# Second parts of w_out by one VectorE subtraction, first parts by ScalarE with the scale

## The chip, the cores and the metric

The kernel runs on one core of a Trainium2 chip. Four engines matter: TensorE (PE in the profile; its weight loads are PEld), VectorE (DVE), ScalarE (ACT) and GpSimd (POOL). SyncE (SP) issues the DMAs. Every engine works through its own queue in order. The metric is the device time of one execution in microseconds.

## The reference

An attention with a threshold, and behind it a feed-forward layer:

```python
scores = scale * np.matmul(q, k.transpose(0, 1, 3, 2))        # 8 batches, 8 heads, 576 x 576
thresh = np.max(scores, axis=-1, keepdims=True) - tau
scores = np.where(scores >= thresh, scores, -1000000000.0)
attn = np.exp(scores - np.max(scores, axis=-1, keepdims=True))
attn = attn / (np.sum(attn, axis=-1, keepdims=True) + 1e-09)
x = np.matmul(attn, v)                                         # as 4608 x 512
h = x @ w_in                                                   # 512 x 2048
g = h * (1.0 / (1.0 + np.exp(-h)))
out = g @ w_out                                                # 2048 x 512
```

## The kernel before

All heavy products but the scores run in float16, each operand as a pair: a first part (the value, scaled by a power of two, rounded to float16) and a second part (what the rounding left). A product is then three matmuls: first by first, first by second, second by first.

**Softmax tiles.** The work is a list of 288 tiles of 128 queries by 576 keys, nine for a pair of heads, 36 for a batch. A tile goes through scores (TensorE, L424, into one of two PSUM buffers s), maximum (VectorE, L434), exponential (ScalarE, L444), mask and sum (VectorE, L453), reciprocal (L461), scaling (ScalarE, L466), first part (GpSimd, L477), second part (GpSimd, L480 and L483), and a DMA transpose into wT. The scores of tile t+2 wait for the mask of tile t, which frees their PSUM. Once the tiles of a pair are transposed, TensorE multiplies them with v (L508, "a"). The pair of v itself is made by ScalarE (L288) and VectorE (L289) and its load needs the buffer that an earlier L289 frees.

**Feed-forward units.** For each batch and range of tokens there are 16 h units (L551: 12 matmuls with w_in, then L559 on ScalarE, L560 on VectorE, L566 on ScalarE, L567 on VectorE, which writes g into gbuf and frees the unit's PSUM bank) and 16 o units (L582: 12 matmuls with w_out each, four units to one of four output blocks; L592 on ScalarE and a DMA write a block). The first range, batch 0 with tokens 0 to 255, has 256 columns and is called h_0_0 and o_0_0; the next, h_0_256, has 320.

**Weights.** w_in and w_out arrive as 64-bit words. Each is 16 pieces of 128 x 512, decoded into float32 slots of the tile wst (L191, L194, L197). When the maxima of a matrix are known, its scale o_w_sc (or i_w_sc) is worked out on VectorE, and split_weights makes the two parts of each piece: L220 scales the piece in place on GpSimd, L223 rounds it to the first part on ScalarE, L224 subtracts on GpSimd. The parts of piece i are written two slots below the piece, over what piece i-2 was; so a first part waits until the second part of the piece two before it has been made. An o unit needs both parts of four pieces.

**Order.** The program calls these steps tile by tile. A plan says at which tile a step of the weights is called (W_PLAN: the scale of w_out is called at place 22 of the tile list and its 16 splits at places 22 to 25; the last field raises the priority of w_out's steps by 150), and how many units are put between the tiles. From these calls and priorities a scheduler that simulates the engines writes each engine's queue, so that an edit in one place reorders the queues from there on.

Of the kernel before, what the change touches and what calls it, by code (L numbers as in the profile page):

```python
# [14 lines left out]
AF = mybir.ActivationFunctionType  # L15
ALU = mybir.AluOpType
# [7 lines left out]
NK = DM // P  # L24
# [28 lines left out]
def attention_moe(  # L53
# [10 lines left out]
    nc = tc.nc  # L64
# [13 lines left out]
    def bank(shape, name, own=None):  # L78
# [10 lines left out]
        out=gate, in0=tau_sb, scalar1=0.0, scalar2=0.125, op0=ALU.is_ge, op1=ALU.mult  # L89
# [3 lines left out]
        out=ntau, in0=tau_sb, scalar1=0.0, scalar2=-1.0, op0=ALU.max, op1=ALU.mult  # L93
# [63 lines left out]
    w16 = wst.bitcast(F16)  # L157
# [58 lines left out]
    def split_weights(i):  # L216
        w = wst[:, i + WSPARE, :]
        hi = w16[:, i, 0:512]
        sc = wsc["in" if i < 4 * NK else "out"][:, 0:1]
        nc.gpsimd.tensor_scalar(  # L220
            out=w, in0=w, scalar1=sc, scalar2=1.0, op0=ALU.mult, op1=ALU.mult
        )
        nc.scalar.activation(hi, w, AF.Copy)  # L223
        nc.gpsimd.tensor_tensor(  # L224
            out=w16[:, i, 512:1024], in0=w, in1=hi, op=ALU.subtract
        )
# [472 lines left out]
    for first, t0, t1, t2, hp in W_PLAN:  # L699
        for i in range(16):  # L700
            ti = t0 + i * (t1 - t0) / 16
            at(math.floor(ti - 2), pri(hp, lambda i=i + first: load_weights(i)))
            at(math.floor(ti), pri(hp, lambda i=i + first: decode_weights(i)))
        at(t1, pri(hp, scale_out if first else scale_in))
        for i in range(16):
            at(t1 + i * (t2 - t1) // 16, pri(hp, lambda i=i + first: split_weights(i)))
# [27 lines left out]
    while t < NT + 8 or units or ready or held:  # L734
# [32 lines left out]
        for v, p, c0, n in avs.pop(t, []):  # L767
# [6 lines left out]
            scale = xscale if v in direct else 2.0**-12  # L774
# [52 lines left out]
```

## Time and profile before

| | |
|---|---|
| median of 3 runs | 1242.41 us (1241.87 to 1245.1) |
| profiled execution, its own time | 1240.96 us |
| its span | 1238.8 us |
| TensorE busy | 1142.8 us, 92% |
| VectorE busy | 931.1 us, 75% |
| ScalarE busy | 814.8 us, 66% |
| GpSimd busy | 748.6 us, 60% |

The page has, in this order, the busy time of each engine, the span in 40 slices (each digit the busy tenths of a slice of 31 us), the DMA queues, the chain of work that ended last, and the costliest groups of instructions: line, engine, operation, output<-inputs, shape, count, busy time and mean ns of one, and the engine's idle time ahead of them with what ended it. The trace behind it also gives the same by windows of time and instruction by instruction. A busy share over the whole span mixes stages with different limits: here the first 213 us, in which weights are decoded and split beside the first tiles, differ from the rest.

### The profile page before, as it was taken

Reading aid. Unit: us, or ns where it says so; the run is one execution under the profiler, and the core shown is the slowest. Engines: PE = TensorE matmul, PEld = TensorE weight load, DVE = VectorE, ACT = ScalarE, POOL = GpSimd, SP = SyncE. Lnnn points to the kernel's source line nnn. Section 1 sums busy time; section 2 is a strip of 40 time slices with the busy share of each in tenths; the row PEclk is TensorE's granted clock in tenths of the full one; section 3 lists DMA queues with packets and bytes.
Section 4 is the critical chain, followed back from the end, with each engine's and each line's share of the span. In section 5 each row is a group of like instructions: output and inputs, shape, how many; then the busy total and the mean of one; then the engine's idle time right before and its main releaser. Section 6 shows DMA issues by size and latency. Waiting matters only on the chain.

```text
span 1238.8 us, 26929 instructions
## 1 busy us (share of the span) xinstructions
PE 1142.8 (92%) x9402; PEld 896.8 (72%) x9402; DVE 931.1 (75%) x2603; ACT 814.8 (66%) x1507; POOL 748.6 (60%) x952
## 2 busy tenths in 40 slices
PE   5776766999899999999999999999999999999998
PEld 3544545777678778777777877787777877777777
DVE  7898866797989998989888859887689848333230
ACT  6888656687677867776777747776677847433331
POOL 1088999788678867886788618783688537200000
PEclk9997887999999999999999999999999999999999
DMA  9669556877878877788787648773688446200000
GB/s 303 183 208 207 129 98 131 158 135 151 163 129 151 160 150 146 154 144 162 141 153 148 123 99 146 157 148 88 118 162 154 83 79 112 52 15 15 14 12 24
DMA packets 363479, 158.15 MB, mean 128 GB/s; under 512 B 329552, under 2 KB 338256, under 8 KB 363344
## 3 DMA queue, kind: packets, MB, share of 16 engines
q1 hardware_dynamic: 363344, 156.43, 62.3%
q8 instruction: 74, 1.21, 0.4%
q14 instruction: 61, 0.50, 0.1%
HBM read 66.72 MB, written 9.44 MB: 61 GB/s over the span
## 4 chain that ended last, share of the span: by engine, by line
PE 64%; DVE 13%; DMA 8%; POOL 5%; ACT 5%; issue 3%; SPq 1%; POOLq 0%; ACTq 0%; DVEq 0%
PE h L551 23%; PE o L582 23%; PE s L424 10%; PE a L508 8%; DMA wT<-hl 3%; DVE w L453 3%; DVE sm L434 3%; DMA vraw<-in_vL 2%; DVE qstack L328 2%; POOL hl L480 2%; ACT w L444 2%; DVE v L289 1%; DMA wraw<-in_w_out 1%; POOL hl L477 1%; ACT w L466 1%
## 5 line engine op out<-in xcount | busy, mean ns | idle before, releaser
L551 PE MATMUL h<-x,wst 128*128 128x288 f16 (+2 forms) x3072 | 430.9, 289 | 14.0 <-DVE gbuf L567 12.0
L582 PE MATMUL o<-gbuf,wst 128*128 128x288 f16 (+2 forms) x3072 | 426.2, 288 | 4.9 <-ACT wst L592 2.5
L551 PEld LDWEIGHTS <-wst 128*128 128x128 f16 x3072 | 292.6, 99 | 102.8 <-issue 22.1
L582 PEld LDWEIGHTS <-wst 128*128 128x128 f16 x3072 | 294.5, 99 | 89.5 <-issue 9.1
L480 POOL TENSOR_TENSOR hl<-w,hl 128x512 f16<-128x512 f32 x272 | 325.3, 1196 | 15.7 <-DMA kraw<-in_kT 3.5
L477 POOL TENSOR_SCALAR hl<-w 128x576 f16<-128x576 f32 x264 | 178.8, 680 | 198.4 <-ACT w L466 128.3
L444 ACT ACTIVATE w<-s,sm 128x576 f32<-128x576 f32 x288 | 210.1, 737 | 81.4 <-DVE sm L434 33.8
L453 DVE SCALAR_TENSOR_TENSOR w<-s,sm,w 128x576 f32<-128x576 f32 x288 | 232.5, 812 | 41.4 <-ACT w L444 39.4
L466 ACT ACTIVATE w<-w,sm 128x576 f32<-128x576 f32 x288 | 218.4, 771 | 58.4 <-DVE sm L461 56.5
L434 DVE TENSOR_REDUCE sm<-s 128x1 f32<-128x576 f32 x288 | 215.0, 750 | 42.8 <-PE s L424 41.0
L560 DVE SCALAR_TENSOR_TENSOR h<-th,h 128x288 f32<-128x288 f32 (+2 forms) x256 | 116.5, 456 | 114.5 <-ACT th L559 112.0
L559 ACT ACTIVATE th<-h,msc 128x288 f32<-128x288 f32 (+2 forms) x256 | 126.9, 497 | 105.4 <-PE h L551 103.0
L424 PE MATMUL s<-khi,qstack 128*128 128x288 f32 x608 | 160.6, 346 | 31.3 <-DVE w L453 27.2
L566 ACT ACTIVATE gbuf<-h 128x288 f16<-128x288 f32 (+2 forms) x256 | 103.7, 407 | 81.6 <-DVE h L560 80.5
L567 DVE SCALAR_TENSOR_TENSOR gbuf<-h,gbuf 128x288 f16<-128x288 f32 (+2 forms) x256 | 114.9, 451 | 40.8 <-ACT gbuf L566 39.8
L508 PE MATMUL a<-wT,v 128*64 128x288 f16 (+1 forms) x1680 | 128.7, 295 | 10.2 <-DMA wT<-hl 10.2
L424 PEld LDWEIGHTS s<-khi,qstack 128*128 128x128 f32 x608 | 98.6, 197 | 53.8 <-issue 42.1
L338 POOL TENSOR_TENSOR klo<-kraw,khi 128x576 fp32r<-128x576 f32 x64 | 92.5, 1446 | 71.3 <-ACT khi L336 71.3
L424 PE MATMUL s<-klo,qstack 128*128 128x288 f32 x608 | 133.7, 302 | 0.0
L508 PEld LDWEIGHTS <-v 128*64 128x64 f16 x1680 | 91.3, 111 | 37.0 <-issue 25.0
L424 PEld LDWEIGHTS s<-klo,qstack 128*128 128x128 f32 x608 | 101.5, 196 | 0.5 <-issue 0.2
L483 POOL TENSOR_TENSOR hl<-w,hl 128x64 f16<-128x64 f32 x272 | 101.7, 374 | 0.0
(93 smaller groups left out, 830.6 us busy)
## 6 DMA issues: line engine op xcount, KB each, us to landing
qraw<-in_qT SPq DMA_DIRECT2D x128, 144.0 KB, 3.0
kraw<-in_kT SPq DMA_DIRECT2D x128, 144.0 KB, 3.1
vraw<-in_vL SPq DMA_DIRECT2D x32, 320.0 KB, 3.4
wraw<-in_w_out SPq DMA_DIRECT2D x16, 512.0 KB, 4.4
out_t<-wst SPq DMA_DIRECT2D x56, 144.0 KB, 2.2
wT<-hl SPq DMA_TRANSPOSE x304, 3.4
gbuf<-in_w_in SPq DMA_DIRECT2D x8, 512.0 KB, 7.5
wraw<-in_w_in SPq DMA_DIRECT2D x8, 512.0 KB, 6.0
```

What stands on the lines that cost most here:

```text
L424: nc.tensor.matmul(s_ps[:, j, :HALF], lhs, kk[:, j * HALF : (j + 1) * HALF], start=(n == 0), stop=(n == len(seq) - 1),)
L434: nc.vector.tensor_reduce(out=negm, in_=s_ps[:, :, :HALF], op=ALU.max, axis=AX.XY, negate=True)
L444: nc.scalar.activation(wtile[t].rearrange("p (j c) -> p j c", j=2), sps[t][:, :, :HALF], AF.Exp, bias=small[t][:, 0:1],)
L453: nc.vector.scalar_tensor_tensor(out=w3, in0=s_ps[:, :, :HALF], scalar=sm[:, 1:2], in1=w3, op0=ALU.is_ge, op1=ALU.mult, accum_out=sm[:, 2:3],)
L466: nc.scalar.activation(w, w, AF.Copy, scale=r)
L477: nc.gpsimd.tensor_scalar(out=fl[:, 0:S], in0=w, scalar1=1.0, scalar2=1.0, op0=ALU.mult, op1=ALU.mult)
L480: nc.gpsimd.tensor_tensor(out=fl[:, 640:1152], in0=w[:, 0:512], in1=fl[:, 0:512], op=ALU.subtract)
L508: nc.tensor.matmul(a_ps[odd * D : (odd + 1) * D, :n], vt[:, lo_v, odd, kv, :], wT[v, b * H + 2 * p + odd][:, kw, c0 - base : c0 - base + n ...
L551: nc.tensor.matmul(ph[:, :n], wi(c, f, lo_w), x16[b, lo_x][:, c, c0 : c0 + n], start=(k == 0), stop=(k == 11),)
L559: nc.scalar.activation(th[:, :n], ph[:, :n], AF.Tanh, scale=moe_sc[b][:, 0:1])
L560: nc.vector.scalar_tensor_tensor(out=ph[:, :n], in0=th[:, :n], scalar=1.0, in1=ph[:, :n], op0=ALU.add, op1=ALU.mult,)
L582: nc.tensor.matmul(ps[:, :n], wo(f, d, lo_w), g[:, lo_g, :n], start=(f == 0 and k == 0), stop=(f == NF - 1 and k == 2),)
```

## The change

For the 16 pieces of w_out the scaling on GpSimd is gone. ScalarE makes the first part from the unscaled piece with the scale as its factor, and VectorE makes the second part in one instruction, piece times scale minus first part. The pieces of w_in are treated as before. The scale is a power of two, so the parts are the same numbers.

```diff
         sc = wsc["in" if i < 4 * NK else "out"][:, 0:1]
+        if i >= 4 * NK:
+            nc.scalar.activation(hi, w, AF.Copy, scale=sc)
+            nc.vector.scalar_tensor_tensor(
+                out=w16[:, i, 512:1024], in0=w, scalar=sc, in1=hi, op0=ALU.mult, op1=ALU.subtract
+            )
+            return
         nc.gpsimd.tensor_scalar(
             out=w, in0=w, scalar1=sc, scalar2=1.0, op0=ALU.mult, op1=ALU.mult
         )
         nc.scalar.activation(hi, w, AF.Copy)
         nc.gpsimd.tensor_tensor(
             out=w16[:, i, 512:1024], in0=w, in1=hi, op=ALU.subtract
         )
```

In the changed file the new instructions are L221 (ScalarE) and L222 (VectorE), and every later line number is six higher: L480 becomes L486, L453 L459, L551 L557, L582 L588.

The queues change from there on. GpSimd before, where tile 42 comes (hl and w32 carry the tile's number, klo is a second part of k; the last number of a name only tells buffers apart):

```order
L477 TENSOR_SCALAR hl_41_1927<-w32_41_1878 128x576
L220 TENSOR_SCALAR wst_89<-wst_89,o_w_sc_996 128x512 x15
L224 TENSOR_TENSOR wst_89<-wst_89 128x512
L220 TENSOR_SCALAR wst_89<-wst_89,o_w_sc_996 128x512
L224 TENSOR_TENSOR wst_89<-wst_89 128x512
L480 TENSOR_TENSOR hl_40_1888<-w32_40_1806,hl_40_1888 128x512
L483 TENSOR_TENSOR hl_40_1888<-w32_40_1806,hl_40_1888 128x64
L480 TENSOR_TENSOR hl_41_1927<-w32_41_1878,hl_41_1927 128x512
L483 TENSOR_TENSOR hl_41_1927<-w32_41_1878,hl_41_1927 128x64
L477 TENSOR_SCALAR hl_42_1975<-w32_42_1917 128x576
```

GpSimd of the change, at the same place:

```order
L483 TENSOR_SCALAR hl_41_1911<-w32_41_1862 128x576
L486 TENSOR_TENSOR hl_40_1872<-w32_40_1790,hl_40_1872 128x512
L489 TENSOR_TENSOR hl_40_1872<-w32_40_1790,hl_40_1872 128x64
L486 TENSOR_TENSOR hl_41_1911<-w32_41_1862,hl_41_1911 128x512
L489 TENSOR_TENSOR hl_41_1911<-w32_41_1862,hl_41_1911 128x64
L483 TENSOR_SCALAR hl_42_1959<-w32_42_1901 128x576
```

The 18 rows of w_out between the first and second parts of tiles 40 and 41 are gone; the tiles follow one another.

VectorE of the change, from its first new subtraction on (th and h belong to an h unit, sm and s to a tile, v16 to a pair of v):

```order
L566 SCALAR_TENSOR_TENSOR h_0_0_8_1138<-th_0_0_8_1175,h_0_0_8_1138 128x256
L222 SCALAR_TENSOR_TENSOR wst_89<-wst_89,o_w_sc_996 128x512
L463 TENSOR_SCALAR sm_42_1900<-sm_42_1900 128x1
L275 TENSOR_TENSOR msc_1_3566<-v1_sc_2117,i_w_sc_584 128x1
L222 SCALAR_TENSOR_TENSOR wst_89<-wst_89,o_w_sc_996 128x512
L566 SCALAR_TENSOR_TENSOR h_0_0_9_1162<-th_0_0_9_1208,h_0_0_9_1162 128x256
L440 TENSOR_REDUCE sm_44_1984<-s_44_1952 128x1
L467 RECIPROCAL sm_42_1900<-sm_42_1900 128x1
```

and its last ones, ahead of the maximum of tile 51:

```order
L459 SCALAR_TENSOR_TENSOR w32_47_2092,sm_47_2091<-s_47_2070,sm_47_2091,w32_47_2092 128x576
L222 SCALAR_TENSOR_TENSOR wst_89<-wst_89,o_w_sc_996 128x512
L459 SCALAR_TENSOR_TENSOR w32_49_2141,sm_49_2140<-s_49_2123,sm_49_2140,w32_49_2141 128x576
L222 SCALAR_TENSOR_TENSOR wst_89<-wst_89,o_w_sc_996 128x512
L463 TENSOR_SCALAR sm_47_2091<-sm_47_2091 128x1
L573 SCALAR_TENSOR_TENSOR gbuf_61<-h_0_0_13_1298,gbuf_61 128x256
L566 SCALAR_TENSOR_TENSOR h_0_0_14_1345<-th_0_0_14_1400,h_0_0_14_1345 128x256
L440 TENSOR_REDUCE sm_50_2153<-s_50_2144 128x1
```

The 16 stand among the work of tiles 42 to 51, and with them the units h_0_0_14 and h_0_0_15 have moved behind those tiles. On TensorE, before, all h_0_0 units and 40 matmuls of o_0_0 stand ahead of the scores of tile 51; in the changed queue h_0_0_15 and all of o_0_0 stand behind them. Ahead of the scores of tile 59 the queue before has 94 matmuls of o_0_0 and 12 of h_0_256, the changed one 153 and 9.

## The prediction

> **What bounds the kernel now.** I read the page's busy shares and slices first.
>
> ```profile
> PE 1142.8 (92%) x9402; PEld 896.8 (72%) x9402; DVE 931.1 (75%) x2603; ACT 814.8 (66%) x1507; POOL 748.6 (60%) x952
> PE   5776766999899999999999999999999999999998
> POOL 1088999788678867886788618783688537200000
> ```
>
> TensorE is at 9 tenths from about 215 us to the end, and short of that in the first seven slices (31 us each). The windows by stage say who is short there; the columns are length, then PE, PEld, DVE, ACT and POOL busy, then granted clock and DMA.
>
> ```profile
> 20.00:40.00 20.00, 13.59 (x64) 8.90 (x64) 19.86 (x55) 18.15 (x37) 1.74 (x2) 0.83 0.86 248
> 60.00:142.00 82.00, 59.30 (x404) 43.76 (x404) 72.15 (x203) 68.91 (x132) 72.61 (x76) 0.83 0.82 192
> 142.00:184.20 42.20, 24.14 (x173) 18.68 (x172) 27.33 (x66) 24.32 (x45) 40.34 (x50) 0.86 0.48 98
> 142.00:213.00 71.00, 43.75 (x295) 33.61 (x294) 47.25 (x119) 42.17 (x74) 67.62 (x80) 0.83 0.54 108
> 213.00:300.00 87.00, 81.40 (x674) 62.62 (x672) 71.96 (x210) 63.21 (x113) 68.89 (x92) 0.98 0.80 151
> 300.00:1100.00 800.00, 781.91 (x6716) 621.42 (x6716) 654.47 (x1859) 553.88 (x1017) 535.99 (x697) 1.00 0.69 131
> ```
>
> From 142 to 213 us GpSimd is busy 67.62 of 71.00 us, TensorE only 43.75, VectorE 0.67 of the time. This is the stage of the edit, and 27.3 us of TensorE's idle time lie in it. After 213 us TensorE is busy 0.94 and then 0.98, so what this stage loses is not made up later. The chain of waits runs through the edited instructions:
>
> ```profile
> 142.02 7.97 POOL wst L220 x11
> ...
> 167.37 5.09 DMA wT<-hl
> ...
> 172.60 3.14 PE a L508 x22
> ...
> 178.44 3.58 DVE v L289
> 182.04 3.22 DMA vraw<-in_vL
> ```
>
> The block of scalings (L220) starts as tile 42 reaches GpSimd; the probabilities of tiles 40 to 42 wait behind it, then their transposes, the product with v, the next v and its load.
>
> **The change, part by part.**
>
> ```profile
> L220 POOL TENSOR_SCALAR wst<-wst,o_w_sc 128x512 f32<-128x512 f32 x16 | 12.5, 798 | 0.0
> L224 POOL TENSOR_TENSOR wst<-wst 128x512 f16<-128x512 f32 x32 | 37.8, 1192 | 0.1
> L223 ACT ACTIVATE wst<-wst 128x512 f16<-128x512 f32 x32 | 19.5, 621 | 0.6 <-POOL wst L224 0.5
> L288 ACT ACTIVATE v<-vraw,v_sc 128x640 f16<-128x640 f32 x32 | 24.5, 817 | 2.0 <-DVE v_sc L146 2.0
> L289 DVE SCALAR_TENSOR_TENSOR v<-vraw,v_sc,v 128x640 f16<-128x640 f32 x32 | 34.2, 1086 | 2.3 <-ACT v L288 2.2
> ```
>
> *Removed from GpSimd:* 16 scalings, 12.5 us, and 16 of the 32 subtractions, 16 x 1.192 = 19.1 us. Of its 67.6 us some 36 remain: it no longer bounds the stage.
>
> *ScalarE:* the first part now takes the scale from a tile, as L288 does: 817 x 512/640 = 654 ns against 621, 0.5 us over 16. At 42.17 of 71.00 us ScalarE hides that; with no cover it costs 0.5 us.
>
> *Added to VectorE:* 16 scaling subtractions. The trace of before has no such instruction on these tiles; L289 has the same operands in 640 columns. Its mean makes 1086 x 512/640 = 0.87 us, so 13.9 us. Bounds:
>
> ```profile
> L197 DVE SCALAR_TENSOR_TENSOR wst<-wraw,wst x24: 677/691/1642, 21.5 to 125.7; 128x512 int32<-128x512 int32 x24
> L289 DVE SCALAR_TENSOR_TENSOR v<-vraw,v_sc,v x4: 868/1272/3568, 143.3 to 199.3; 128x640 f16<-128x640 f32 x4
> 142.00:213.00 71.00, 6.98 (x4) 0.83 0.54 108
> ```
>
> The floor is the shortest L197 (min/median/max ns), 0.68 us; the ceiling is the longest L289, 3.568 x 0.8 = 2.85 us. The four L289 of this stage took 6.98 us (last row, that line alone), 1.40 us each at 512 columns. I take 0.87: the long ones fell where GpSimd ran without a gap, which the change ends.
>
> *Moved.* In the changed VectorE queue the 16 stand spread before the reduction of tile 51. Behind it go two L567, an L560 and an L453; ahead of it comes an L251. By the means of these rows that is 0.812 + 2 x 0.451 + 0.456 - 0.811 = 1.4 us less.
>
> ```profile
> L453 DVE SCALAR_TENSOR_TENSOR w<-s,sm,w 128x576 f32<-128x576 f32 x288 | 232.5, 812 | 41.4 <-ACT w L444 39.4
> L560 DVE SCALAR_TENSOR_TENSOR h<-th,h 128x288 f32<-128x288 f32 (+2 forms) x256 | 116.5, 456 | 114.5 <-ACT th L559 112.0
> L567 DVE SCALAR_TENSOR_TENSOR gbuf<-h,gbuf 128x288 f16<-128x288 f32 (+2 forms) x256 | 114.9, 451 | 40.8 <-ACT gbuf L566 39.8
> L251 DVE TENSOR_REDUCE vmx<-vraw 128x1 f32<-128x640 f32 x32 | 25.9, 811 | 11.0 <-DMA vraw<-in_vL 11.0
> ```
>
> *First half, 142 us to tile 51* (reduction at 184.20 us, row below). VectorE: 27.33 + 13.9 - 1.4, less 2.5 for the one L289 of 3.57 us at its mean: 37.3 us. When VectorE is the fullest engine beside a working GpSimd it is busy 72.15/82 = 0.88 (window 60 to 142). 37.3/0.88 = 42.4 us against 42.2: tile 51 comes 0.2 us later.
>
> *Second half, tile 51 to tile 59.*
>
> ```profile
> 153.08 2.80 PE L551 MATMUL h<-x,wst 128*128 128x256 f16 x24 [2.01 <-DVE gbuf L567]
> 156.51 2.80 PE L551 MATMUL h<-x,wst 128*128 128x256 f16 x24 [0.63 <-DVE gbuf L567]
> ...
> 193.75 2.09 PE L508 MATMUL a<-wT,v 128*64 128x320 f16 x28
> ...
> 196.28 0.49 PE L424 MATMUL s<-khi,qstack 128*128 128x288 f32 x2
> 196.62 0.42 PE L424 MATMUL s<-klo,qstack 128*128 128x288 f32 x2
> 196.88 1.27 PE L582 MATMUL o<-gbuf,wst 128*128 128x256 f16 x10
> ...
> 184.20 0.76 DVE L434 TENSOR_REDUCE sm<-s 128x1 f32<-128x576 f32 x1 [0.34 <-PE s L424]
> ...
> 212.99 0.76 DVE L434 TENSOR_REDUCE sm<-s 128x1 f32<-128x576 f32 x1 [0.56 <-PE s L424]
> ```
>
> The changed TensorE queue has there 153 matmuls of o and 12 of h, 28 of a and 36 of s. At 2.80/24 = 0.117 us, 2.09 us in all, and 0.60 us per four (196.28 to 196.88): 19.3 + 2.1 + 5.4 = 26.8 us. All parts of w_out exist by then, so TensorE bounds; at 81.40/87 = 0.936 busy that is 28.6 us. I add one wait of 2.0 us (row 153.08): the last h units' L567 now stand behind tile 51. Together 30.6 against 28.8: tile 59 comes 2.0 us later than before.
>
> *Work done by tile 59.* The queue before has 94 matmuls of o and 12 of h_0_256 ahead of tile 59, the changed one 153 and 9: 56 more, 56 x 0.117 = 6.6 us that need not be done later.
>
> *Sum:* 6.6 - 2.0 = 4.6 us gained. The profiled execution, 1240.96 us (span 1238.8 and 2.2 around it), becomes 1236.4; the median shown, 1.4 us higher, becomes 1237.8. It reaches the end because TensorE is busy 781.91 of 800 us from 300 us on.
>
> **Queue and port.** On VectorE's queue, behind each new subtraction, stand the masks and sums of the softmax tiles, whose PSUM the next scores wait for; behind each ScalarE first part, which waits for the subtraction two parts back (it overwrites that one's source), stand exponentials. That is the 0.88. As for contention, the long L289 (178.44 us, 3.58) ran beside these:
>
> ```profile
> 178.81 1.15 POOL L480 TENSOR_TENSOR hl<-w,hl 128x512 f16<-128x512 f32 x1
> ...
> 180.18 1.14 POOL L480 TENSOR_TENSOR hl<-w,hl 128x512 f16<-128x512 f32 x1
> 181.29 0.88 POOL L483 TENSOR_TENSOR hl<-w,hl 128x64 f16<-128x64 f32 x1
> ```
>
> The Trainium skill (SBUF — State Buffer, Who interferes with whom) says that a VectorE instruction with two SBUF inputs and a GpSimd one that reads SBUF exclude each other, the later blocking for the whole of the other. By that rule, the trace agrees: L289 got through only after two L480, and the L483 that met it took 0.88 us. An estimate by the rule: GpSimd busy 36/71 of the time, half an L480 left on average, 0.30 us on the floor of 0.68, 0.98 each; 1.8/0.88 = 2.0 us less gain, 1239.8 us.
>
> **Rivals.**
>
> *Contention, slower.* Each subtraction costs what the stage's own L289 did, 1.40 us, and L289 stays long: 16 x 0.53 + 2.5 = 11.0 us more, over 0.88 is 12.5 us: 4.6 - 12.5, 7.9 us slower, 1250.3. It decides from 0.87 + 4.6 x 0.88/16 = 1.12 us per subtraction. For it: the 6.98 us above. Against it: GpSimd falls to half busy, and the L289 of the whole run average 1.09 us with GpSimd busy 535.99 of 800 us. The rule named above is this mechanism at 0.98 us, short of the deciding point; the 1.12 us would be reached where GpSimd, behind a wait, works its queue off without a gap. The ceiling of 2.85 us would make 36 us more; it needs a GpSimd without gaps, and I leave it out.
>
> *Ping-pong, no change.* ScalarE and VectorE wait for each other through the alternating parts, and VectorE reaches only half way from its 0.67 in this stage to 0.88, 0.775: 37.3/0.775 = 48.1 us, 5.7 more: 1.1 us slower, 1243.5. For it: the parts go in pairs, each pair bound to the one before. Against it: 20 to 40 us has the two engines alternating over the same tiles at 19.86 of 20.
>
> *Denser, faster still.* VectorE at 0.99 as in 20 to 40 us and subtractions at the floor: (27.33 + 10.9 - 1.4 - 2.7)/0.99 = 34.5 us, 7.9 less: 12.5 us gained, 1229.9. Against it: GpSimd was nearly idle then.
>
> **How the numbers follow.** Chances: forecast 0.45, ping-pong 0.28, contention 0.19, denser 0.08. About 0.3%, 3.7 us, is what a measurement of this kernel tells from no change. The forecast's own range, 1234 to 1240, lies nearly all below 1238.7: 0.42 of its 0.45 count as faster, with denser 0.50. Ping-pong gives 0.25 to the same, with the forecast's rest 0.28; the other 0.03 with contention make slower 0.22. The range reaches from denser, 1229, into contention, 1247; it leaves out some 0.04 below and 0.14 above.
>
> **What would show it.** Right: GpSimd near 36 us between 142 and 213, the subtractions near 0.87 us, VectorE near 0.88 busy up to tile 51, scores of tile 59 near 215 us with o units mostly done, TensorE near 0.94 from tile 51 on. Wrong: subtractions above 1.12 us, tile 51 after 190 us, or more TensorE idle time after 300 us than the 18 of before, which would mean that the new order gives the gain back.

## The result and the profile after

The changed kernel took 1228.88 us (median of 4 runs, 1228.62 to 1229.91) beside 1242.22 for the kernel before: a ratio of 0.9889 with a 95% interval of 0.9872 to 0.9906, so 1.1% faster. A later comparison with 10 runs of it and 27 of before gave 1230.77 against 1240.60, 0.9930 (0.9913 to 0.9948). The two intervals do not meet; the gain is 10 to 13 us, where the prediction had 4.6. All ratios compare fast executions alone: one slow execution, of the kernel called "w_in too" below, took 1659.59 us at a granted clock of 0.654 and is left out of its ratio.

The page of the changed kernel, busy shares and slices. VectorE is up by 8.5 us and GpSimd down by 24.2. TensorE is at 7 and 9 tenths in slices 6 and 7, where before had 6 in both, and at 8 or 9 behind them:

```profile
PE 1142.7 (93%) x9402; PEld 896.0 (73%) x9402; DVE 939.6 (77%) x2619; ACT 816.1 (66%) x1507; POOL 724.4 (59%) x920
PE   5876779999889999998999999999999999999998
```

Windows of the changed kernel. The first two stretches run from the maximum of tile 42 (135.0 us; 135.8 before) to that of tile 51 and on to tile 59; the others are the fixed ones of the prediction. The tile list has empty places, so that VectorE takes eight maxima from tile 42 to 51 and eight from there to 59.

```profile
135.00:176.90 41.90, 26.40 (x172) 19.78 (x169) 41.74 (x100) 31.17 (x57) 27.86 (x29) 0.78 0.56 124
176.90:204.40 27.50, 27.17 (x237) 23.07 (x236) 21.52 (x64) 18.56 (x30) 22.96 (x29) 0.97 0.83 153
142.00:213.00 71.00, 55.79 (x431) 44.69 (x431) 62.59 (x156) 49.26 (x83) 51.23 (x61) 0.86 0.69 139
213.00:300.00 87.00, 84.71 (x683) 62.68 (x681) 77.17 (x223) 63.76 (x113) 66.33 (x86) 1.00 0.82 154
300.00:1100.00 800.00, 776.23 (x6658) 618.30 (x6657) 645.07 (x1833) 549.09 (x1013) 529.73 (x688) 0.99 0.67 128
```

The same two stretches of the kernel before:

```profile
135.80:184.20 48.40, 29.67 (x219) 23.01 (x218) 33.53 (x89) 28.77 (x54) 46.38 (x57) 0.88 0.49 99
184.20:213.00 28.80, 19.61 (x123) 14.93 (x124) 19.92 (x54) 17.85 (x30) 27.27 (x31) 0.78 0.62 122
```

The first stretch has changed hands. GpSimd was busy 46.38 of 48.40 us there; now VectorE is busy 41.74 of 41.90, and in the list of waits for that stretch VectorE has no entry at all. In the second TensorE is busy 27.17 of 27.50 us, before 19.61 of 28.80. TensorE's idle time from 142 to 213 us falls from 27.2 to 15.2 us and from 213 to 300 us from 5.6 to 2.3; from 300 to 1100 us it rises from 18.1 to 23.8.

The maxima of tiles 51 and 59 in the changed kernel (VectorE's timeline), 184.20 and 212.99 us before:

```profile
176.87 0.73 DVE L440 TENSOR_REDUCE sm<-s 128x1 f32<-128x576 f32 x1
...
204.37 0.74 DVE L440 TENSOR_REDUCE sm<-s 128x1 f32<-128x576 f32 x1
```

The chain of waits of the changed kernel at the place of the scaling block (start, us, work). Where GpSimd stood with L220, VectorE now stands with L222 between its other work:

```profile
140.92 0.96 DVE wst L222
141.94 0.97 DVE msc L275
142.90 0.80 DVE wst L222
...
144.99 2.01 DVE v L295 x2
...
147.46 0.73 DVE w L459 x2
148.19 1.33 DVE wst L222 x2
```

The new groups, with the idle time ahead of them behind the last bar:

```profile
L222 DVE SCALAR_TENSOR_TENSOR wst<-wst,o_w_sc 128x512 f16<-128x512 f32 x16 | 14.5, 924 | 0.0
L221 ACT ACTIVATE wst<-wst,o_w_sc 128x512 f16<-128x512 f32 x16 | 11.3, 721 | 4.7 <-DVE wst L222 4.5
```

VectorE never waited ahead of a subtraction. ScalarE waited 4.5 us in all for the subtraction two pieces back; VectorE, full all the while, did not have to wait for it.

### The profile page after: what moved, and what is told of

Read it like the earlier page. It is cut to its first block, busy times and chain, and to the rows that moved or that the text cites. A ratio compares the mean times of both kernels' runs of the same rounds, so it can differ in the third digit from the quotient of the medians.

```text
span 1228.1 us, 26910 instructions
## 1 busy us (share of the span) xinstructions
PE 1142.7 (93%) x9402; PEld 896.0 (73%) x9402; DVE 939.6 (77%) x2619; ACT 816.1 (66%) x1507; POOL 724.4 (59%) x920
## 4 chain that ended last, share of the span: by engine, by line
PE 61%; DVE 17%; DMA 7%; ACT 5%; POOL 5%; issue 4%; SPq 1%; ACTq 0%; POOLq 0%; DVEq 0%
PE o L588 22%; PE h L557 22%; PE s L430 9%; PE a L514 7%; DVE w L459 3%; DVE sm L440 3%; DMA wT<-hl 3%; DVE qstack L334 2%; DMA vraw<-in_vL 2%; POOL hl L486 2%; POOL hl L483 1%; ACT w L450 1%; DVE v L295 1%; ACT w L472 1%; DVE h L566 1%
## 5 line engine op out<-in xcount | busy, mean ns | idle before, releaser
L557 PE MATMUL h<-x,wst 128*128 128x288 f16 (+2 forms) x3072 | 435.8, 291 | 21.7 <-DVE gbuf L573 20.6
L588 PE MATMUL o<-gbuf,wst 128*128 128x288 f16 (+2 forms) x3072 | 421.5, 287 | 2.6 <-ACT wst L598 2.0
L557 PEld LDWEIGHTS <-wst 128*128 128x128 f16 x3072 | 293.3, 99 | 114.5 <-issue 31.7
L588 PEld LDWEIGHTS <-wst 128*128 128x128 f16 x3072 | 293.7, 98 | 84.3 <-issue 6.4
L486 POOL TENSOR_TENSOR hl<-w,hl 128x512 f16<-128x512 f32 x272 | 329.7, 1212 | 14.5 <-DMA kraw<-in_kT 1.8
L459 DVE SCALAR_TENSOR_TENSOR w<-s,sm,w 128x576 f32<-128x576 f32 x288 | 231.7, 813 | 30.3 <-ACT w L450 28.0
L573 DVE SCALAR_TENSOR_TENSOR gbuf<-h,gbuf 128x288 f16<-128x288 f32 (+2 forms) x256 | 115.6, 453 | 45.4 <-ACT gbuf L572 44.7
L430 PEld LDWEIGHTS s<-khi,qstack 128*128 128x128 f32 x608 | 97.6, 195 | 42.5 <-issue 29.6
```

Source lines behind the costliest of these rows:

```text
L430: nc.tensor.matmul(s_ps[:, j, :HALF], lhs, kk[:, j * HALF : (j + 1) * HALF], start=(n == 0), stop=(n == len(seq) - 1),)
L459: nc.vector.scalar_tensor_tensor(out=w3, in0=s_ps[:, :, :HALF], scalar=sm[:, 1:2], in1=w3, op0=ALU.is_ge, op1=ALU.mult, accum_out=sm[:, 2:3],)
L486: nc.gpsimd.tensor_tensor(out=fl[:, 640:1152], in0=w[:, 0:512], in1=fl[:, 0:512], op=ALU.subtract)
L557: nc.tensor.matmul(ph[:, :n], wi(c, f, lo_w), x16[b, lo_x][:, c, c0 : c0 + n], start=(k == 0), stop=(k == 11),)
L588: nc.tensor.matmul(ps[:, :n], wo(f, d, lo_w), g[:, lo_g, :n], start=(f == 0 and k == 0), stop=(f == NF - 1 and k == 2),)
```

## The experiments

Two theories stand first. **Load**: the gain is GpSimd time taken out of the stage, which VectorE then fills without a gap. **Place**: what counts is the block of scalings in GpSimd's queue, ahead of tile 42 and all behind it. A third, **order**, says that the gain is chance of newly written queues. In the table, us from tile 42 to 51 and from 51 to 59 are taken at the maxima on VectorE; the idle columns are TensorE's, length less busy time of the windows. All of these lengths are good to about 0.1 us. Behind the first two rows stand three groups of four kernels, each group on another chip, with the runs of before that it shares: 1240.83, then 1240.60, then 1240.64; across groups, compare the ratios. The columns behind the ratio come from one profiled execution of each kernel, not always a typical one: that of "changed, again" took 1237.41 us, that of "every fourth piece mixed" 1226.38.

| kernel | median | ratio to before (95%) | 42 to 51 | 51 to 59 | idle 142–213 | 213–300 | 300–1100 |
|---|---|---|---|---|---|---|---|
| before | 1242.22 | 1 | 48.4 | 28.8 | 27.2 | 5.6 | 18.1 |
| changed | 1228.88 | 0.9889 (0.9872–0.9906) | 41.9 | 27.5 | 15.2 | 2.3 | 23.8 |
| scaling to ScalarE alone | 1236.64 | 0.9961 (0.9945–0.9978) | 38.1 | 38.3 | 24.8 | 2.0 | 20.7 |
| subtraction to VectorE alone | 1239.73 | 0.9988 (0.9968–1.0008) | 48.1 | 25.9 | 16.2 | 5.6 | 27.0 |
| subtraction twice | 1237.05 | 0.9962 (0.9947–0.9978) | 47.8 | 32.7 | 20.3 | 5.5 | 25.3 |
| no subtraction | 1227.01 | 0.9875 (0.9848–0.9902) | 35.5 | 26.0 | 11.3 | 5.4 | 19.2 |
| changed, again | 1230.77 | 0.9930 (0.9913–0.9948) | 43.1 | 27.8 | 17.8 | 2.2 | 23.2 |
| changed, 0.96 | 1233.40 | 0.9940 (0.9919–0.9962) | 42.5 | 28.1 | 17.1 | 2.3 | 25.1 |
| before, 0.96 | 1242.49 | 1.0015 (0.9999–1.0031) | 48.6 | 28.3 | 27.7 | 5.9 | 18.3 |
| w_in too | 1234.76 | 0.9950 (0.9932–0.9968) | 43.5 | 24.6 | 11.8 | 5.4 | 22.2 |
| changed, 0.85 | 1230.24 | 0.9917 (0.9897–0.9937) | 42.6 | 28.0 | 16.1 | 2.1 | 23.2 |
| before, 0.85 | 1239.66 | 1.0005 (0.9984–1.0026) | 47.7 | 29.5 | 25.4 | 6.3 | 18.7 |
| changed, 0.90 | 1230.81 | 0.9918 (0.9903–0.9933) | 43.9 | 27.8 | 15.5 | 2.7 | 25.1 |
| every fourth piece mixed | 1230.10 | 0.9922 (0.9903–0.9940) | 40.5 | 27.0 | 15.9 | 5.4 | 19.0 |

### Each half alone

First the scaling alone, then the subtraction alone:

```diff
+        if i >= 4 * NK:
+            nc.scalar.activation(w, w, AF.Copy, scale=sc)
+            nc.scalar.activation(hi, w, AF.Copy)
+            nc.gpsimd.tensor_tensor(
+                out=w16[:, i, 512:1024], in0=w, in1=hi, op=ALU.subtract
+            )
+            return
```

> Half of the change: for w_out the scaling leaves GpSimd (ScalarE scales the piece in place, one instruction more per piece), the subtraction stays on GpSimd and VectorE gets nothing. Theory load (the gain is GpSimd time taken out of the stage 142 to 213 us, which VectorE then fills without a gap): GpSimd has 12.5 us less, 55 of 71; I expect 6 to 10 us of the 13 gained, 1232 to 1236 us. Theory place (the 15 scalings in one block ahead of tile 42 hold up the chain; the rest of the load does not matter): the block is gone, so the whole gain or more, 1226 to 1230 us. Theory order (the gain is chance of the new queue order): anywhere within 5 us of either kernel.

```diff
         nc.scalar.activation(hi, w, AF.Copy)
-        nc.gpsimd.tensor_tensor(
+        (nc.vector if i >= 4 * NK else nc.gpsimd).tensor_tensor(
             out=w16[:, i, 512:1024], in0=w, in1=hi, op=ALU.subtract
         )
```

> The other half: for w_out GpSimd scales in place as before, the block of 15 included, and VectorE makes the subtraction without a scale. Theory load: GpSimd has 18.3 us less, 49 of 71, VectorE some 12 us more; 6 to 10 us gained, 1232 to 1236 us. Theory place: the block still stands ahead of tile 42, so little or nothing gained, 1238 to 1243 us.

Measured: 4.2 us and 1.1 us gained (the second not told from none), 5.3 together against 10 to 13 for both. 1236.64 us lies outside what either the load or the place theory asked for; 1239.73 is what the place theory asked for. Both fit the order theory, whose range takes in nearly everything between the two kernels, so that the totals do not test it. The windows say more. Scaling alone, from tile 42 to 51 and from 51 to 59:

```profile
136.40:174.50 38.10, 21.58 (x154) 17.72 (x151) 28.72 (x81) 34.94 (x66) 33.25 (x36) 0.82 0.63 129
174.50:212.80 38.30, 29.72 (x217) 23.59 (x217) 28.26 (x66) 22.57 (x38) 31.98 (x40) 0.82 0.58 107
```

Without the block the tiles run ahead, 38.1 us instead of 48.4, with ScalarE the fullest at 34.94; that is the place theory's part. But the second stretch lasts 38.3 us instead of 28.8: what was won first is lost there. The 16 subtractions remain on GpSimd, seven of them behind tile 51, and it is still 0.87 and 0.84 busy. The longest piece of the chain of waits in that stretch is one VectorE instruction, which prepares operands of later scores (VectorE's timeline):

```profile
183.90 6.59 DVE L335 SCALAR_TENSOR_TENSOR qstack<-qraw,gate,qstack 64x576 fp32r<-64x576 f32 x1
```

The shortest of its line takes 0.82 us. GpSimd, with two of the subtractions among its work, ran without a gap while this one lasted, until 189.87 us, and it ended 0.6 us later; the next mask and the scores that needed it waited behind it. That is 5.8 of the 9.5 us lost, and the same pattern as the long L289 of the prediction (3.6 to 4.7 us in the three kernels of before). With the subtractions off GpSimd, in the changed kernel and in the one with the subtraction alone, no VectorE instruction that starts between 142 and 213 us lasts over 2 us. Subtraction alone:

```profile
136.90:185.00 48.10, 33.15 (x236) 26.49 (x237) 43.57 (x107) 32.42 (x62) 45.13 (x51) 0.86 0.53 114
185.00:210.90 25.90, 25.90 (x226) 21.70 (x225) 20.89 (x58) 18.31 (x30) 20.39 (x27) 1.00 0.85 151
```

GpSimd is at 45.13 of 48.10 us and tile 51 as late after tile 42 as before: the block does hold the tiles. TensorE meanwhile did more units (33.15 us against 29.67), and behind tile 51 it is never idle. So the idle time of 142 to 213 us falls to 16.2 us, nearly as with the whole change, but 32.6 us follow up to 1100 us where before had 23.7, and the end keeps 1 us. By these windows and rows both parts of GpSimd's load have to go: the block for the first stretch, the subtractions for the second. Why this kernel loses 9 us more behind 213 us was not found; its waits there are spread over transposes and VectorE's small instructions.

### Twice, and not at all

```diff
             nc.vector.scalar_tensor_tensor(
                 out=w16[:, i, 512:1024], in0=w, scalar=sc, in1=hi, op0=ALU.mult, op1=ALU.subtract
             )
+            nc.vector.scalar_tensor_tensor(
+                out=w16[:, i, 512:1024], in0=w, scalar=sc, in1=hi, op0=ALU.mult, op1=ALU.subtract
+            )
```

> The changed kernel with each of the 16 VectorE subtractions done twice, the same result written again. Theory load with VectorE as the bound of the stage up to tile 51: 16 x 0.75 to 0.9 us more VectorE time, all of it on the path: tile 51's maximum moves from 177 to 189 us and the end by 9 to 13 us, 1238 to 1242 us. If VectorE still had gaps to fill, as my 0.88 assumed (5 us of them in 42), the end moves by 7 us or less, below 1236 us.

For the other, those lines are taken out, and wo() returns the first part in the place of the second, so that the kernel leaves out the second parts of w_out:

> The changed kernel without the 16 subtractions at all: second parts of w_out are not made, and the third matmul of each o product uses the first part instead, so the same number of matmuls runs on other numbers. Theory load with VectorE as the bound: 14 us less on VectorE, but TensorE's own 28 us of work before tile 51 and the softmax chain take over: 5 to 12 us faster than the changed kernel, 1217 to 1224 us. If TensorE or the softmax chain already bounds the stage in the changed kernel: within 3 us of 1229 us.

Twice: 6 to 8 us above the medians of the changed kernel, 4 to 9 us by the ratios. That does not decide between the two readings; the window from tile 42 to 51 does:

```profile
136.50:184.30 47.80, 30.00 (x195) 22.86 (x196) 47.63 (x110) 31.02 (x56) 26.88 (x29) 0.79 0.54 114
```

VectorE is again without a gap (47.63 of 47.80), the stretch is 5.9 us longer and the next 5.2: 11.1 us of the 15 us added come out at tile 59, so VectorE bounds. Of the 32 subtractions, which took 30.3 us, 22 stand ahead of tile 51 in this queue and 10 behind it, hence not the 12 us in the first stretch that I had written. Not at all:

```profile
134.60:170.10 35.50, 23.60 (x155) 18.25 (x156) 30.06 (x84) 30.83 (x57) 27.73 (x33) 0.81 0.74 156
```

The stretch to tile 51 is 6.4 us shorter than in the changed kernel, and VectorE, at 30.06 of 35.50 us, has gaps again. The end comes 2 to 4 us earlier by the medians, 2 to 7 by the ratios, of which the smaller is not told from none; the 5 to 12 expected are neither met nor excluded. On one and the same chip the two kernels, with 32 subtractions and with none, are 10.0 us apart: of 30.3 us of VectorE's work a third reaches the end; what took up the rest was not followed.

### Is it chance of the order, and what comes back later?

> The changed kernel once more, so that the others of this set stand beside it on one chip: 13 us (1.1%) faster than before, 1227 to 1230 us.

> The changed kernel with the number of feed-forward units per tile from batch 1 on raised from 0.95 to 0.96 of an even spread. The queues up to 213 us stay nearly as they are, those behind are written anew. TensorE's idle time from 300 to 600 us is 19.9 us in the changed kernel, 11.4 before. Theory order: that rise is chance of the order, so this kernel's own value lies anywhere from 11 to 20 us and its time within 6 us of 1229. Theory limit: TensorE arrives there ahead of the tiles and is held by VectorE, so 18 to 22 us idle again, and the time within 2 us of 1229.

> The same 0.96 in the kernel before. Theory order: idle from 300 to 600 us anywhere from 11 to 20 us, the time within 6 us of 1242. Theory limit: 10 to 13 us idle, within 2 us of 1242. Either way the stage from 142 to 213 us keeps its 27 us of TensorE idle time.

With `RATE = 0.96` the queues change only from about 800 us on, which I had not seen when I wrote these; the order could not move the idle time of 300 to 600 us (19.2 us changed, 11.9 before), so these two only repeat the comparison: 1233.40 against 1242.49. The next three reorder VectorE's queue in some 1000 rows: `RATES = (1.3, 0.85)` in both kernels, `RATE = 0.90` in the changed one.

> The changed kernel with 0.85 instead of 0.80 feed-forward units per tile in the last part of batch 0 (the second entry of RATES). The queues up to 240 us stay; from there on some 1000 rows of VectorE's queue differ, where 0.96 had changed 316, and those only from about 800 us on, so that it could not tell the theories apart for 300 to 600 us. TensorE's idle time from 300 to 600 us is 18.7 to 19.9 us in the changed kernel, 11.4 to 11.9 in the kernel before. Theory order: this value moves by 4 us or more either way. Theory limit (TensorE comes there ahead and VectorE holds it): 17 to 21 us again. By the first the time lies anywhere from 5 us below the changed kernel to 3 above.

> The same 0.85 in the kernel before. Theory order: its 11.4 us of idle time from 300 to 600 us move by 4 us or more, more likely up. Theory limit: 10 to 13 us, and the time within 2 us of before.

> The changed kernel with 0.90 instead of 0.95 of an even spread of units from batch 1 on; VectorE's queue differs in 970 rows, from about 350 us on. Theory order: 300 to 600 us idle anywhere from 11 to 23 us. Theory limit: 17 to 21 us; the units held back make it no shorter.

The gain repeats: the five changed kernels have 41.9 to 43.9 us from tile 42 to 51 and 15.2 to 17.8 us idle from 142 to 213, the three of before 47.7 to 48.6 and 25.4 to 27.7. But these kernels do not test the order inside that stage. In their traces the instructions of every engine come in the same order as in the changed kernel (or the one before) up to 280 us or later. That the gain is no chance of the order there rests on kernels whose queues differ in the stage: two that follow below keep it (every fourth piece mixed, 40.5 us and 15.9 idle; w_in too, 43.5 and 11.8), and so does the one without subtractions (35.5 and 11.3).

What comes back later is mixed. From 300 to 600 us the changed kernel is idle 19.9, 18.7, 19.2, 16.1 and 13.5 us, before 11.4, 11.9 and 10.7. The 13.5 of 0.90 fits the order theory alone, the 10.7 of before with 0.85 the limit theory alone, and the 16.1 lies between them. Over 300 to 1100 us the sum hardly moves with these orders: 23.8, 23.2, 25.1, 23.2, 25.1 against 18.1, 18.3, 18.7, some 5 us more. Counted from 213 us, with the stretch in which TensorE gained 3 to 4 us, it is 25.3 to 27.8 against 23.7 to 25.0, some 2 us more. Kernels with another order in the stage need not show it: with every fourth piece mixed the idle time behind 300 us is 19.0. Why it comes back is not shown. The reordered kernels were not told from the changed one in time.

### Further in the same direction

w_in treated the same way (the condition is taken out):

```diff
-        if i >= 4 * NK:
+        if i >= 0:
```

> The changed kernel with the pieces of w_in treated in the same way. Their split runs at 68 to 140 us, where VectorE is busy 0.90 and GpSimd 0.90 in the changed kernel. Theory load with VectorE as the bound: 12 to 14 us more VectorE work there, of which 8 us of gaps can hold some: 3 to 8 us slower than the changed kernel, 1232 to 1237 us. If GpSimd bounds that stage as it did the next one: 3 to 10 us faster, 1219 to 1226 us.

4 us above the changed kernel of the same group, as the load theory asked. Its window from 60 to 142 us:

```profile
60.00:142.00 82.00, 56.41 (x381) 40.88 (x379) 75.46 (x212) 70.22 (x133) 38.20 (x41) 0.83 0.74 190
```

GpSimd falls from 73.69 us there to 38.20 and TensorE does not gain by it (56.41 us after 60.12 in the changed kernel and 58.31 in "changed, again"): GpSimd, though 0.90 busy, was not the limit. That VectorE was, at 75.46 of 82 us, is argued. Where the 4 us are lost the profiles do not show: up to 213 us TensorE is idle 58.5 us in this kernel and 58.8 in "changed, again".

A quarter of the pieces of w_out made by ScalarE and GpSimd as in the first experiment (`if i % 4 == 3`), the others as changed:

> The changed kernel, but for every fourth piece of w_out ScalarE scales in place, copies, and GpSimd subtracts; VectorE makes 12 of the 16. In the changed kernel VectorE has no gap from tile 42 to tile 51 (41.74 of 41.90 us) while ScalarE is busy 31.2 and GpSimd 27.9. Theory load with VectorE as the bound: 4 x 0.92 = 3.7 us less VectorE work, ScalarE and GpSimd still below 0.9: tile 51 two to four us earlier, the time 1 to 4 us below the changed kernel. If ScalarE's longer chain per piece takes over, as where it scaled all 16: 0 to 4 us above it.

Tile 51 comes after 40.5 us instead of 41.9 to 43.9, with VectorE still full:

```profile
135.00:175.50 40.50, 23.48 (x172) 18.61 (x171) 40.34 (x95) 33.34 (x62) 32.08 (x34) 0.86 0.63 135
```

The time, 1230.10, is not told from that of the changed kernel, whose medians are 1228.88 and 1230.77. Of the 3.7 us of VectorE's work that were to go, only some 1.7 went: its 12 subtractions took 12.8 us, 1.07 each instead of 0.92, beside a GpSimd that was now busy 32.08 of 40.50 us.

## Why the prediction was right and wrong

**GpSimd bounds the stage, and VectorE takes over up to tile 51, TensorE behind it: right.** The windows show each. GpSimd's 36 us from 142 to 213 us came out as 51.23, because the tiles run ahead: 18 of their first parts start in that window instead of 14.

**The price of a subtraction, 0.87 us: about right.** It was 0.924 us on average, 14.5 in all. The contention rival needed 1.12. Its mechanism exists: eleven took 0.73 to 0.79 us, five 0.87 to 1.84, and the longest ran into GpSimd. VectorE's timeline first, then GpSimd's:

```profile
152.03 1.84 DVE L222 SCALAR_TENSOR_TENSOR wst<-wst,o_w_sc 128x512 f16<-128x512 f32 x1
```

```profile
151.39 1.93 POOL L344 TENSOR_TENSOR klo<-kraw,khi 128x576 fp32r<-128x576 f32 x1 [3.11 <-ACT khi L342]
```

The subtraction ended 0.5 us after the GpSimd instruction that had started first. That agrees with the rule of the Trainium skill that the prediction cited (SBUF — State Buffer, Who interferes with whom); its estimate of 0.98 us was 0.06 high, as far off as mine was low. The L289 of the prediction shows more than one turn lost: it began at 178.44 us, while an L224 ran until 178.84, and got through only after two L480 that had started later. Nor is the price the same in every kernel: 0.96 and 0.99 us for the two sets of the kernel that subtracts twice, 1.07 with every fourth piece mixed, near the contention rival's 1.12.

**VectorE's share of 0.88 up to tile 51: wrong, and the step that failed.** It was 0.996. I had taken 0.88 from the stage before, where both VectorE and GpSimd were at 0.88, and read it as what VectorE can reach beside a working GpSimd. It was no ceiling here: with the subtractions, whose first parts ScalarE had ready each time (idle ahead of them 0.0), VectorE had work at every moment. Doubling them left the share at 0.996, and without them it fell to 0.85. Tile 51 was forecast 0.2 us late and came 7.3 us early. From 142 us to it, in the changed kernel:

```profile
142.00:176.87 34.87, 20.83 (x124) 15.46 (x124) 34.71 (x76) 24.91 (x45) 21.03 (x21) 0.73 0.55 124
```

Two thirds of the miss are the share: 37.3 us of work at 0.996 make 37.4 us instead of 42.4. The other 2.6 us are the work itself, 34.7 us instead of 37.3: its parts other than subtractions took 21.2 us, not 23.4, and one subtraction came ahead of 142 us. The 0.996 is the "denser" rival's 0.99, which got a chance of 0.08 because GpSimd had been nearly idle where the row came from. GpSimd's load did not keep the share down; it entered by the price, since a subtraction that is held up counts as busy. That this rival's 1229.9 us is close to the time measured is partly luck: its price of 0.68 us was too low, its second half 3 us too long, and it had nothing coming back later.

**The second half, 30.6 us: too long by 3.** It took 27.5. My 26.8 us of TensorE work were about right (27.17); the 0.936 was 0.99, and the added wait of 2.0 us did not come in it. The waits for L573 fell in the first half, 10.8 us of them, where VectorE and not TensorE set the pace.

**Work ahead at tile 59, 6.6 us: about right.** TensorE has been busy 149.31 us when the maximum of tile 59 begins, before 144.11: 5.2 us of work more, 8.6 us earlier. The early gain is 13.8 us by these, 15.2 by my own 6.6, where I had 4.6; TensorE's idle time from 142 to 300 us is less by 15.3 us (17.5 against 32.8).

**That it reaches the end:** only in part. 10.7 us of span remain of some 15 at 300 us, and some 5 us came back between 300 and 1100 us. I had named this as a sign of error and given it no price; it made the forecast look less wrong than its first term was.

**Place.** The chain showed the block of scalings ahead of tile 42, and I priced it only as part of GpSimd's sum. The two halves show that it has an effect of its own: without it tile 51 comes 10 us earlier even with the subtractions still on GpSimd, with it not at all.

## What to carry to other kernels

An engine's busy share in a neighbouring stage is not its ceiling: ask whether the queue will hold work that is ready at every moment, and if the added instructions are such work, take 1.0 for the bound. When an engine is relieved of two kinds of work, each kind can hold another stretch, and the halves can be worth less than the whole. A gain made early need not all reach the end: here a third of what TensorE had gained by 300 us came back as idle time, for a reason that was not found, and it should be given a price.

## What the runs showed of the hardware

An activation whose scale comes from a tile took 721 ns for 512 columns (L221; 706 at least). The same instruction without a scale from a tile took 624 ns in the same kernel. Nor is the time proportional to the columns: the 817 ns for 640 columns (L288 before) would have made 654. The scale from a tile cost 1.6 us over the 16, and they lay beside other work.

VectorE ran 42 us at 0.996 while GpSimd, in the same stretch, was busy two thirds of the time.

One VectorE instruction with two tiles as inputs lasted until GpSimd paused, 0.6 us past the end of its work: L335 took 6.59 us in the kernel with the scaling alone, where the shortest of its line took 0.82.
